# Attention outputs kept chunk by chunk, and their tail columns stored from a small copied tile

## The chip, the core and the metric

The kernel runs on one core of a Trainium2 chip. The core has TensorE (PE: matmuls; PEld: the loads of the stationary operand), VectorE (DVE), ScalarE (ACT), GpSimd (POOL) and SyncE (SP), each with its own queue of instructions, and 16 DMA engines that serve the transfers which SP, ACT and POOL issue. The metric is the device time of the whole program in microseconds. Three runs of the kernel before gave 4875.46, 4877.3 and 4885.39 us; the median is 4877.3 us.

## The reference

Four layers act on x of 2048 rows by 640 columns: A, B, A, B, each added to x after a layer norm. Layer A is the one that the change touches. It cuts the rows into 64 segments of 32, puts 8 memory rows in front of each, and runs attention with 32 heads of 192 columns over the 40 rows; the outputs of the memory rows are the memory of the next segment, so that the segments follow one another:

```python
for s in range(n_seg):
    h = jnp.concatenate([mem, xs], axis=1)          # 8 + 32 rows
    q, k, v = (einsum('btd,dhe->bhte', h, W) for W in (Wq, Wk, Wv))
    p = softmax(where(mask, q @ k.T * scale, -1e9))
    o = einsum('bhte,hed->btd', p @ v, Wo)          # 40 rows of 640
    mem = o[:, :M, :]
    outs.append(o[:, M:, :])
```

Layer B is a linear attention with learned features; it is not changed, apart from the rows of layer A that it finishes at its start.

## The kernel before, in words

**Two parts of a layer A.** A_pre computes queries, keys and values for the last 8 rows of every segment at once and leaves them in DRAM (kqb, vb). A_chain then walks through the 64 segments with the other 32 rows (8 memory rows and 24 rows of x). Each segment has four rounds of 8 heads (NR = 4, L = 3). A round needs Q, K and V of the 32 rows (project, L940: 20 matmuls each, in four column tiles of the array), takes the last 8 rows' columns from DRAM, and computes scores, weights (E), their sums, and attend.

**What a round holds.** The 8 heads are split into two groups, G. A round's attention output is six chunks of 128 partitions, and each chunk has 80 columns: 64 for the 32 rows of the two groups ("main"), 16 for their last 8 rows ("tail"). By the parity of the round the order is main then tail or tail then main, so that a round's new tail columns don't fall where the last round's are still in use.

**OT.** scale_out (L1007) divides attend's result in PSUM by the sums and writes OT, in three VectorE instructions: L1012 for the chunks 0 to 3 (128 x 320 elements) and L1016 twice for the halves of chunks 4 and 5 (64 x 160). OT is `[P, 96, 6]`: slots (columns) outside, the six chunks inside, so that neighbours of one chunk lie six elements apart. Of its 96 slots a round writes 80, from slot 16 or from slot 0 by parity; the main columns are always slots 16 to 79, the tail is 80 to 95 or 0 to 15. There is one OT.

**Who reads OT.** wo_round (L1023) multiplies the main columns by Wo: 12 steps of four matmuls, steps 0 to 7 with the chunks 0 to 3, steps 8 to 11 with the chunks 4 and 5; all four rounds of a segment accumulate in one PSUM tile, W. store_tail (L1018) sends the 16 tail slots to DRAM (otb) in a DMA that GpSimd issues straight from OT. to_raw (L945) also borrows OT's main slots, as a place for the raw K of round 0, before the transposes spread it.

**The tail's V rows.** extra_v (L921) is a DMA, issued by GpSimd, from vb into 16 rows of Vp; attend reads all 96 rows of Vp, so an attend waits until it has landed, and it is issued once the attend before is done.

**The order in a segment** is written out by hand (L1060 to L1160, manual schedule). On TensorE: Q0, K0, Q1, V0, scores 0, K1; then for n = 1, 2: Q(n+1), sums, attend(n-1), scores(n), K(n+1), V(n), and for n = 1 wo_round 0; then V3, sums, attend 2, scores 3, wo_round 1, sums, attend 3, wo_round 2, wo_round 3. scale_out of round n - 1 stands on VectorE between the transposes of Q(n+1) and K(n+1) (for n = 2 behind those of K). On GpSimd, in one queue: extra_v, the four copies and the load of kqb for the next round (L910 to L919), store_tail, and once a segment the store of the rows of the segment before (attn, L906) and the load of the next rows (xr, L890). At a segment's end 25 single-column weight loads (L1035) fill TensorE, VectorE transposes the memory rows of W into hT (L1158, L1159), and the next segment's Q0 begins. The attends of a segment are counted 0 to 3 here.

**The tail's product with Wo** follows in layer B: post_steps fetches otb for 16 segments, spread (L1174) lays each round's tail out as 12 chunks of 128 columns in two copies, one on VectorE and one on ScalarE, and multiply runs the matmuls. The first spreads run while the last segment of the chain is still under way.

Of the kernel before, what the change touches and what calls it, by code (L numbers as in the profile page):

```python
# [8 lines left out]
P = 128  # L9
BF16 = mybir.dt.bfloat16  # L10
F32 = mybir.dt.float32
ACT = mybir.ActivationFunctionType
ALU = mybir.AluOpType
# [102 lines left out]
class Kernel:  # L116
# [746 lines left out]
    def A_chain(self, xn_dram, at_dram, li, load_slot, piece, load_wo, late_wo, wo_mid, wo_end, low):  # L863
        nc, tc, KC, NSEG = self.nc, self.tc, self.KC, self.NSEG
        scale = float(self.Dh) ** -0.5
        NR = 4
        with tc.tile_pool(name=f"A{li}_ch", reuse_waits="tile", bufs=1) as sp, \
# [3 lines left out]
            KT = sp.tile([P, 6, 96], BF16, name="KT")  # L871
            QT = sp.tile([P, 2, 4, 80], BF16, name="QT")
            Vs = sp.tile([P, 896], BF16, name="Vp")
            OT = sp.tile([P, 96, 6], BF16, name="OT")
            for i, t in enumerate((KT, QT, Vs)):
                (nc.vector if i % 2 else nc.gpsimd).memset(t[:], 0.0)
            at_rows = self.attn_rows
# [1 line left out]
            def rounds(s):  # L879
                return range(NR) if s % 2 == 0 else range(NR - 1, -1, -1)  # L880
# [40 lines left out]
            def extra_v(s, n):  # L921
                r = rounds(s)[n]
                t = 64 + 16 * (n % 2)
                nc.gpsimd.dma_start(out=Vs[t:t + 16, :], in_=self.vb_d[s, r].rearrange("g t f -> (g t) f"))  # L924
# [18 lines left out]
                        load_slot(m, order[NR - 1], b)  # L943

            def to_raw(ps, spare):  # L945
                raw = OT[:, 16:80, :].rearrange("p q c -> p (q c)") if spare else sp.tile([P, 384], BF16, name="raw", tag="raw")[:, :]
                nc.scalar.activation(out=raw, in_=ps[:, 0:384], func=ACT.Copy)  # L947
                return raw

# [54 lines left out]
                                         stop=(k == 192), skip_group_check=True)  # L1004
                return O

            def scale_out(O, rc, n):  # L1007
                q0 = 16 - 16 * (n % 2)
                dst = OT[:, q0:q0 + 80, :].rearrange("p q c -> p c q")
                rv = rc[:, :].rearrange("p (x e q) -> p x e q", e=2, q=80)  # L1010
                ov = O[:, 0:480].rearrange("p (c q) -> p c q", q=80)
                nc.vector.tensor_tensor(out=dst[:, 0:4, :], in0=ov[:, 0:4, :],  # L1012
                                        in1=rc[:, :].rearrange("p (c q) -> p c q", q=80), op=ALU.mult)
                for e in range(2):
                    h = slice(64 * e, 64 * e + 64)
                    nc.vector.tensor_tensor(out=dst[h, 4:6, :], in0=ov[h, 4:6, :], in1=rv[h, :, e, :], op=ALU.mult)  # L1016

            def store_tail(n, s, r):  # L1018
                q0 = 80 - 80 * (n % 2)
                nc.gpsimd.dma_start(out=self.otb_d[s, :, 96 * r:96 * r + 96],  # L1020
                                    in_=OT[:, q0:q0 + 16, :].rearrange("p q c -> p (q c)"))

            def wo_round(W, r, first, last):  # L1023
                w = wo_end[:, :] if r in (0, 3) else wo_mid[:, 7680 * (r - 1):7680 * r]
                for i in range(12):
                    G, c = (i // 4, i % 4) if i < 8 else (i % 4 // 2, 4 + i % 2)
                    for g in range(4):
                        nc.tensor.matmul(W[32 * g:32 * g + 32, 0:160], lhsT=OT[:, 16 + 32 * G:48 + 32 * G, c],  # L1028
                                         rhs=w[:, 640 * i + 160 * g:640 * i + 160 * g + 160], start=(first and i == 0),
                                         stop=(last and i == 11), tile_position=(0, 32 * g), skip_group_check=True)  # L1030

# [26 lines left out]
            W = None  # L1058
            for s in range(NSEG):
                order = rounds(s)  # L1060
                L = NR - 1

                def q_or_k(m, n):
                    ps = pqp.tile([P, 512], F32, name="ps_qk", tag="qk")
                    project(hT, ps, m, n, s)
                    return to_raw(ps, m == "K" and n == 0)

                def values(n, pool, tag):
                    pv = pool.tile([P, 512], F32, name="ps_v", tag=tag)
                    project(hT, pv, "V", n, s)  # L1070
                    return pv

                def tails_after(n):
                    if n + 2 < NR:
                        extra_v(s, n + 2)
                    elif s + 1 < NSEG:
                        extra_v(s + 1, n + 2 - NR)

                raw = q_or_k("Q", 0)
                if s > 0:  # L1080
                    io = keep_rows(W)
                to_rows(raw, "Q")
                if s == 0:
                    fill(FILL[li])
                to_rows(q_or_k("K", 0), "K")
                if s == 0:
                    late_wo(2)
                if s > 0:
                    store_rows(s - 1, io)
                W = pop.tile([P, 512], F32, name="ps_w", tag="w")  # L1090
                raw = q_or_k("Q", 1)
                pv = values(0, pop, "v")
                v_rows(pv, 0, "s")
                v_rows(pv, 1, "s")
                S = scores(0)
                to_rows(raw, "Q", 1)
                next_kq(s, 0)
                E = weigh(S)
                to_rows(q_or_k("K", 1), "K")
                if s + 1 < NSEG:  # L1100
                    xr = load_rows(s + 1)
                for n in range(1, L):
                    raw = q_or_k("Q", n + 1)
                    sums(S, E)
                    O = attend(E)
                    tails_after(n - 1)
                    S1 = scores(n)
                    rc = reciprocals(S)
                    E = weigh(S1)
                    S = S1  # L1110
                    to_rows(raw, "Q", n + 1)
                    next_kq(s, n)
                    if n == L - 1:
                        to_rows(q_or_k("K", n + 1), "K")
                        scale_out(O, rc, n - 1)
                    else:
                        rawk = q_or_k("K", n + 1)
                        scale_out(O, rc, n - 1)
                        to_rows(rawk, "K")
                    store_tail(n - 1, s, order[n - 1])  # L1120
                    pv = values(n, pop, "v")
                    v_rows(pv, 0, "s")
                    v_rows(pv, 1, "s")
                    if n < L - 1:
                        wo_round(W, order[n - 1], n == 1, False)
                        if n == 1:
                            load_wo(order[L])
                            if s == NSEG - 1:
                                load_wo(3, low[:, 0:7680])
                pv = values(L, pqp, "qk")  # L1130
                sums(S, E)
                O = attend(E)
                tails_after(L - 1)
                S1 = scores(L)
                next_kq(s, L)
                rc = reciprocals(S)
                E = weigh(S1)
                v_rows(pv, 1, "v")
                v_rows(pv, 0, "s")
                wo_round(W, order[L - 2], False, False)  # L1140
                sums(S1, E)
                O1 = attend(E)
                tails_after(L)
                if s + 1 < NSEG:
                    hT = new_hT()
                    hx_transpose(hT, xr)
                scale_out(O, rc, L - 1)
                store_tail(L - 1, s, order[L - 1])
                wo_round(W, order[L - 1], False, False)
                rc = reciprocals(S1)  # L1150
                scale_out(O1, rc, L)
                wo_round(W, order[L], False, True)
                store_tail(L, s, order[L])
                fill(SEG_FILL)
                if s + 1 < NSEG:
                    wt = sp.tile([P, KC, 32], F32, name="wt", tag="raw")
                    for b0, b1 in ((2, 5), (0, 2)):
                        nc.vector.transpose(out=wt[:, b0:b1, :], in_=W[:, 0:160].rearrange("p (j b) -> p b j", b=KC)[:, b0:b1, :])  # L1158
                        nc.vector.tensor_copy(out=hT[:, b0:b1, 0:8], in_=wt[:, b0:b1, 0:8])  # L1159
            store_rows(NSEG - 1, keep_rows(W))  # L1160

    def post_steps(self, ops):

        nc = self.nc
# [9 lines left out]
        def spread(tb, ot):  # L1174
            o = 7680 + 12288 * (tb % 2)
            ow = low[:, o + 6144:o + 12288].rearrange("p (c q) -> p c q", q=P)
            for k in range(4):
                o5 = ow[:, 12 * k:12 * k + 12, :].rearrange("p (c g) (s t) -> p g c s t", g=2, t=8)
                i5 = ot[:, :, 96 * k:96 * k + 96].rearrange("p s (g t c) -> p g c s t", g=2, c=6)
                for g in range(2):  # L1180
                    self.ev.copy(out=o5[:, g], in_=i5[:, g], eng="vs"[g])
            return ow

        def multiply(tb, ow, p0, p1):
# [49 lines left out]
```

## Time and profile before

| What | Value |
|---|---|
| Median of three runs | 4877.3 us |
| The profiled execution, its own time | 4893.74 us |
| Its span, first to last instruction | 4892.0 us |
| Mean granted TensorE clock | 0.873 |
| Busy: PE, DVE, ACT, POOL | 3831.1, 2763.4, 1971.6, 1719.9 us |
| OT written on VectorE (L1012 and L1016) | 628.8 + 781.7 us |
| One segment of the chain, mean of 126 | 30.60 us |

How to read the lines that follow. In a group of instructions the order is: line of the kernel, engine, operation, output<-inputs with shapes, count | busy us in total, mean ns of one | idle us of the engine just before, and what ended it. In the list of waits it is: engine, tile and line that waited <- what it waited for: us in total, times, longest. In a timeline it is: start us, duration us, engine, line, operation, and in brackets the idle time before and its releaser. In a table of stretches it is: from:to, length, busy us (and instructions) of PE, PEld, DVE, ACT and POOL, granted clock, DMA share, GB/s.

A timeline merges neighbours of one line, so one entry can be two instructions or 48 matmuls, and the durations overlap where an engine starts the next before the last has ended. The granted clock changes between full and half in windows of 3.41 us. The end of a DMA isn't a line of the timeline; it shows as what a later instruction waited for.

### The profile page before, as it was taken

The numbers are of one execution on the slowest core, as the hardware profiler recorded it, in microseconds if no ns is written. First come the engines' busy times: TensorE is split into PE (matmuls) and PEld (weight loads), VectorE is DVE, ScalarE is ACT, GpSimd is POOL, SyncE is SP. The second block draws the span as 40 slices with busy tenths as digits, with TensorE's granted clock in tenths as the row PEclk, the third lists the DMA queues.
The fourth block names the chain that finished last, engine by engine and source line by source line (L and its number), as shares of the span: only waits on it lengthen the run. The fifth ranks groups of instructions, "written<-read, shape, count | busy, mean of one in ns | idle before, by whom it ended". The sixth has DMA issues, their size and how long they took to land.

```text
span 4892.0 us, 167816 instructions
## 1 busy us (share of the span) xinstructions
PE 3831.1 (78%) x69306; PEld 2480.7 (51%) x72670; DVE 2763.4 (56%) x5448; ACT 1971.6 (40%) x4405; POOL 1719.9 (35%) x4359
## 2 busy tenths in 40 slices
PE   9877777777777777788898777777777777777888
PEld 7544444444454444455466544444444544444554
DVE  5455555555555555556633555555555555555555
ACT  2343343433334333345433444434434444433453
POOL 3333333333333333332242333333333333333310
PEclk9988888888888888889999898888888888888899
DMA  9866666666656555570277566666666666666700
GB/s 296 290 199 199 199 199 198 199 199 199 198 196 200 189 190 194 191 254 23 98 226 243 198 214 197 200 201 199 199 197 200 199 199 199 200 199 199 235 8 22
DMA packets 539947, 934.62 MB, mean 191 GB/s; under 512 B 149554, under 2 KB 307978, under 8 KB 539194
## 3 DMA queue, kind: packets, MB, share of 16 engines
q1 hardware_dynamic: 428858, 818.87, 49.8%
q0 software_dynamic: 76672, 91.77, 6.9%
q10 hardware_dynamic: 33664, 13.24, 1.1%
q8 instruction: 558, 9.14, 0.8%
q14 instruction: 195, 1.60, 0.1%
HBM read 853.72 MB, written 73.40 MB: 190 GB/s over the span
## 4 chain that ended last, share of the span: by engine, by line
issue 29%; PE 25%; POOL 15%; DMA 13%; DVE 9%; ACT 5%; PEld 3%; POOLq 0%; DVEq 0%; SPq 0%; ACTq 0%
DMA Vp<-vb 9%; PE ps_qk L940 8%; DVE OT L1016 6%; PE ps_pre L825 3%; POOL kqb L910 3%; POOL otb L1020 2%; PE ps_o L1002 2%; POOL Vp L924 2%; PEld L1035 2%; DMA attn<-orow 2%; PE ps_w L1028 2%; PE ps_pre L849 1%; POOL KT L919 1%; POOL QT L916 1%; PE ps_qk L391 1%
## 5 line engine op out<-in xcount | busy, mean ns | idle before, releaser
L940 PE MATMUL ps_qk<-arena,hT 128*32 128x384 bf16 x20480 | 1184.8, 385 | 80.7 <-PE L1035 75.7
L940 PEld LDWEIGHTS <-hT 128*32 128x32 bf16 x30720 | 862.1, 109 | 631.9 <-issue 262.2
L1028 PE MATMUL ps_w<-arena,OT 128*32 128x160 bf16 x24576 | 729.6, 269 | 355.0 <-DVE OT L1012 244.3
L947 ACT ACTIVATE raw<-ps_qk 128x384 bf16<-128x384 f32 x896 | 439.2, 490 | 1365.5 <-PE ps_qk L940 1153.5
L1028 PEld LDWEIGHTS <-OT 128*32 128x32 bf16 x24576 | 541.4, 131 | 528.6 <-DVE OT L1012 322.5
L956 DVE STREAM_TRANSPOSE QT<-raw 128x256 bf16<-128x256 bf16 x512 | 228.1, 446 | 1015.3 <-PE ps_s L977 749.2
L1016 DVE TENSOR_TENSOR OT<-ps_o,rc 64x160 bf16<-64x160 f32 x1024 | 781.7, 763 | 13.8
L1012 DVE TENSOR_TENSOR OT<-ps_o,rc 128x320 bf16<-128x320 f32 x512 | 628.8, 1228 | 151.7 <-ACT rc L994 75.1
L1002 PE MATMUL ps_o<-E,Vp 96*128 96x80 bf16 x4096 | 248.1, 209 | 519.9 <-DMA Vp<-vb 463.6
L1020 POOL DMA_DIRECT2D otb<-OT x512 | 281.8, 550 | 922.0 <-DVE OT L1016 898.5
L940 PE MATMUL ps_v<-arena,hT 128*32 128x384 bf16 x10240 | 540.6, 354 | 10.6 <-DMA arena<-in_A_Wv_dram 10.6
L1002 PEld LDWEIGHTS <-Vp 96*128 96x128 bf16 x4096 | 201.9, 103 | 595.9 <-ACT rc L994 267.5
L964 ACT ACTIVATE Vp<-ps_v 64x384 bf16<-64x384 f32 x896 | 433.2, 483 | 117.4 <-PE ps_v L940 90.1
L924 POOL DMA_DIRECT2D Vp<-vb x512 | 258.2, 504 | 535.3 <-PE ps_o L1002 520.1
L994 ACT ACTIVATE rc<-ps_s 128x320 f32<-128x320 f32 x512 | 223.9, 437 | 358.2 <-DVE OT L1016 348.7
L910 POOL DMA_DIRECT2D kqb<-kqb x512 | 292.5, 571 | 158.7 <-POOL KT L919 150.2
L983 ACT ACTIVATE E<-ps_s 96x320 bf16<-96x320 f32 x512 | 220.1, 430 | 294.7 <-PE ps_s L977 291.2
L952 DVE STREAM_TRANSPOSE KT<-raw 128x384 bf16<-128x384 bf16 x384 | 222.1, 578 | 185.6 <-ACT raw L947 181.7
L977 PE MATMUL ps_s<-QT,KT 128*96 128x80 bf16 (+1 forms) x3072 | 259.2, 225 | 8.1 <-DVE KT L952 0.9
L993 ACT ACTIVATE ps_s<-ps_s 128x320 f32<-128x320 f32 x512 | 218.7, 427 | 110.8 <-PE ps_s L988 105.6
L977 PEld LDWEIGHTS <-KT 128*96 128x96 bf16 x3072 | 236.5, 131 | 39.2 <-issue 32.2
L906 POOL DMA_DIRECT2D attn<-orow x128 | 93.0, 726 | 406.3 <-ACT orow L902 405.9
(149 smaller groups left out, 4603.0 us busy)
## 6 DMA issues: line engine op xcount, KB each, us to landing
arena<-wo_rows SPq DMA_DIRECT2D x792, 320.0 KB, 5.5
arena<-in_A_Wq_dram SPq DMA_DIRECT2D x427, 384.0 KB, 4.4
arena<-in_A_Wv_dram SPq DMA_DIRECT2D x427, 384.0 KB, 6.2
arena<-in_A_Wk_dram SPq DMA_DIRECT2D x768, 192.0 KB, 5.0
kqb<-kqb POOLq DMA_DIRECT2D x512, 48.0 KB, 4.3
arena<-in_A_Wk_dram SPq DMA_DIRECT2D x43, 384.0 KB, 7.0
vb<-arena POOLq DMA_DIRECT2D x128, 112.0 KB, 6.0
Vp<-vb POOLq DMA_DIRECT2D x512, 28.0 KB, 4.1
```

The costliest lines, as they stand in the source:

```text
L910: nc.gpsimd.dma_start(out=kqb[:], in_=self.kqb_d[s, :, r, :])
L924: nc.gpsimd.dma_start(out=Vs[t:t + 16, :], in_=self.vb_d[s, r].rearrange("g t f -> (g t) f"))
L940: nc.tensor.matmul(ps[32 * g:32 * g + 32, 0:384], lhsT=hT[:, b, :], rhs=rhs, start=(i == 0), stop=(i == KC - 1), tile_position=(0, 32 * g) ...
L947: nc.scalar.activation(out=raw, in_=ps[:, 0:384], func=ACT.Copy)
L956: nc.vector.transpose(out=QT[:, :, 0:4:3, q:q + 64], in_=rv[:, :, 0:3:2, :])
L964: nc.scalar.activation(out=o, in_=i, func=ACT.Copy)
L977: nc.tensor.matmul(S[0:96, c0:c0 + 80 * (q1 - q0)], lhsT=KT[:, 3 * x + i, :], rhs=QT[:, x, q0:q1, :], start=False, stop=(x == 1 and i == 2 ...
L1002: nc.tensor.matmul(O[:, 80 * c:80 * c + 80], lhsT=Vs[0:96, 448 * x + k:448 * x + k + 128], rhs=E[0:96, 160 * x + 80 * e:160 * x + 80 * e + ...
L1012: nc.vector.tensor_tensor(out=dst[:, 0:4, :], in0=ov[:, 0:4, :], in1=rc[:, :].rearrange("p (c q) -> p c q", q=80), op=ALU.mult)
L1016: nc.vector.tensor_tensor(out=dst[h, 4:6, :], in0=ov[h, 4:6, :], in1=rv[h, :, e, :], op=ALU.mult)
L1020: nc.gpsimd.dma_start(out=self.otb_d[s, :, 96 * r:96 * r + 96], in_=OT[:, q0:q0 + 16, :].rearrange("p q c -> p (q c)"))
L1028: nc.tensor.matmul(W[32 * g:32 * g + 32, 0:160], lhsT=OT[:, 16 + 32 * G:48 + 32 * G, c], rhs=w[:, 640 * i + 160 * g:640 * i + 160 * g + 16 ...
```

## The change

OT becomes `[P, 6, 80]`: chunks outside, the round's 80 columns inside, so that each chunk is a run of 80. The three instructions of scale_out write runs. The main columns now begin at column 0 or 16 of a run by parity (m0 in wo_round), and the tail at 64 or 0. A round's tail is now inside the area that the next round writes. The tail is no longer contiguous, so GpSimd copies its 6 x 16 columns to a tile of 96 elements per partition (otb, one buffer), and the DMA goes from there. The raw K of round 0 goes to the buffer of rc, now widened in its type but not in bytes. The tail's order in DRAM becomes chunk, group, row, so that spread needs one copy of 12 chunks per round and not two of 6; the copies take turns on the two engines.

```diff
-            OT = sp.tile([P, 96, 6], BF16, name="OT")
+            OT = sp.tile([P, 6, 80], BF16, name="OT")
...
             def to_raw(ps, spare):
-                raw = OT[:, 16:80, :].rearrange("p q c -> p (q c)") if spare else sp.tile([P, 384], BF16, name="raw", tag="raw")[:, :]
+                w, tag = (640, "rc") if spare else (384, "raw")
+                raw = sp.tile([P, w], BF16, name="raw", tag=tag)[:, 0:384]
...
-            def scale_out(O, rc, n):
-                q0 = 16 - 16 * (n % 2)
-                dst = OT[:, q0:q0 + 80, :].rearrange("p q c -> p c q")
+            def scale_out(O, rc):
...
-                nc.vector.tensor_tensor(out=dst[:, 0:4, :], in0=ov[:, 0:4, :],
+                nc.vector.tensor_tensor(out=OT[:, 0:4, :], in0=ov[:, 0:4, :],
                                         in1=rc[:, :].rearrange("p (c q) -> p c q", q=80), op=ALU.mult)
                 for e in range(2):
                     h = slice(64 * e, 64 * e + 64)
-                    nc.vector.tensor_tensor(out=dst[h, 4:6, :], in0=ov[h, 4:6, :], in1=rv[h, :, e, :], op=ALU.mult)
+                    nc.vector.tensor_tensor(out=OT[h, 4:6, :], in0=ov[h, 4:6, :], in1=rv[h, :, e, :], op=ALU.mult)
 
             def store_tail(n, s, r):
-                q0 = 80 - 80 * (n % 2)
-                nc.gpsimd.dma_start(out=self.otb_d[s, :, 96 * r:96 * r + 96],
-                                    in_=OT[:, q0:q0 + 16, :].rearrange("p q c -> p (q c)"))
+                q0 = 64 - 64 * (n % 2)
+                ob = sp.tile([P, 96], BF16, name="otb", tag="otb")
+                nc.gpsimd.tensor_copy(out=ob[:, :].rearrange("p (c q) -> p c q", q=16), in_=OT[:, :, q0:q0 + 16])
+                nc.gpsimd.dma_start(out=self.otb_d[s, :, 96 * r:96 * r + 96], in_=ob[:, :])
 
-            def wo_round(W, r, first, last):
+            def wo_round(W, n, r, first, last):
+                m0 = 16 * (n % 2)
...
-                        nc.tensor.matmul(W[32 * g:32 * g + 32, 0:160], lhsT=OT[:, 16 + 32 * G:48 + 32 * G, c],
+                        nc.tensor.matmul(W[32 * g:32 * g + 32, 0:160], lhsT=OT[:, c, m0 + 32 * G:m0 + 32 * G + 32],
...
-                o5 = ow[:, 12 * k:12 * k + 12, :].rearrange("p (c g) (s t) -> p g c s t", g=2, t=8)
-                i5 = ot[:, :, 96 * k:96 * k + 96].rearrange("p s (g t c) -> p g c s t", g=2, c=6)
-                for g in range(2):
-                    self.ev.copy(out=o5[:, g], in_=i5[:, g], eng="vs"[g])
+                self.ev.copy(out=ow[:, 12 * k:12 * k + 12, :].rearrange("p c (s t) -> p c s t", t=8),
+                             in_=ot[:, :, 96 * k:96 * k + 96].rearrange("p s (c t) -> p c s t", t=8))
```

The calls of scale_out and wo_round change their arguments and nothing else; their order stays.

More of the change, by code (lines that the diff above doesn't have):

```diff
@@ L1114, in A_chain @@
                         to_rows(q_or_k("K", n + 1), "K")
-                        scale_out(O, rc, n - 1)
+                        scale_out(O, rc)
                     else:
                         rawk = q_or_k("K", n + 1)
-                        scale_out(O, rc, n - 1)
+                        scale_out(O, rc)
                         to_rows(rawk, "K")
@@ L1124, in A_chain @@
                     if n < L - 1:
-                        wo_round(W, order[n - 1], n == 1, False)
+                        wo_round(W, n - 1, order[n - 1], n == 1, False)
                         if n == 1:
@@ L1139, in A_chain @@
                 v_rows(pv, 0, "s")
-                wo_round(W, order[L - 2], False, False)
+                wo_round(W, L - 2, order[L - 2], False, False)
                 sums(S1, E)
@@ L1146, in A_chain @@
                     hx_transpose(hT, xr)
-                scale_out(O, rc, L - 1)
+                scale_out(O, rc)
                 store_tail(L - 1, s, order[L - 1])
-                wo_round(W, order[L - 1], False, False)
+                wo_round(W, L - 1, order[L - 1], False, False)
                 rc = reciprocals(S1)
-                scale_out(O1, rc, L)
-                wo_round(W, order[L], False, True)
+                scale_out(O1, rc)
+                wo_round(W, L, order[L], False, True)
                 store_tail(L, s, order[L])
```

## The prediction

> **What bounds the kernel now.** I read the page first, then the waits, the groups by shape, one end of a segment as a timeline, and a table of clock windows. The page:
>
> ```profile
> span 4892.0 us, 167816 instructions
> PE 3831.1 (78%) x69306; PEld 2480.7 (51%) x72670; DVE 2763.4 (56%) x5448; ACT 1971.6 (40%) x4405; POOL 1719.9 (35%) x4359
> issue 29%; PE 25%; POOL 15%; DMA 13%; DVE 9%; ACT 5%; PEld 3%; POOLq 0%; DVEq 0%; SPq 0%; ACTq 0%
> DMA Vp<-vb 9%; PE ps_qk L940 8%; DVE OT L1016 6%; PE ps_pre L825 3%; POOL kqb L910 3%; POOL otb L1020 2%; PE ps_o L1002 2%; POOL Vp L924 2%; PEld L1035 2%; DMA attn<-orow 2%; PE ps_w L1028 2%; PE ps_pre L849 1%; POOL KT L919 1%; POOL QT L916 1%; PE ps_qk L391 1%
> ```
>
> No engine is full; the chain hops between a small DMA (Vp<-vb), TensorE, VectorE's OT and GpSimd. So a change is worth what it takes from the wait that ends last, and the busy sum of VectorE says little. The waits name two families in front of TensorE:
>
> ```profile
> PE ps_o L1002 <- DMA Vp<-vb: 463.6, 280, 4.1
> ACT rc L994 <- DVE OT L1016: 348.7, 236, 1.9
> PE ps_w L1028 <- DVE OT L1012: 244.3, 265, 1.3
> PE ps_w L1028 <- DVE OT L1016: 102.2, 222, 0.5
> ```
>
> I then averaged the start times in the trace over the 126 segments of the two recurrent chains that follow one another without a break (30.60 us each, 3855 us of the span). In each, attend 1 and attend 2 start 0.14 us after the tail rows of V land (5th to 95th percentile 0.136 to 0.17 us), and attend 3 does in most (0.14 at the median, 0.55 at the 95th). Their mean starts are 15.72, 21.77 and 25.15 us after the segment's start. So two thirds of a segment is paced by a DMA that GpSimd issues after the previous attend, not by VectorE. Only from attend 3 to the end does OT set the pace.
>
> **What the change does to OT's writes.** The groups by shape:
>
> ```profile
> L1016 DVE TENSOR_TENSOR OT<-ps_o,rc 64x160 bf16<-64x160 f32 x1024 | 781.7, 763 | 13.8
> L1012 DVE TENSOR_TENSOR OT<-ps_o,rc 128x320 bf16<-128x320 f32 x512 | 628.8, 1228 | 151.7 <-ACT rc L994 75.1 <-ACT Vp L964 41.7 <-issue 24.6
> L425 DVE TENSOR_TENSOR arena<-ps_v,rk 128x320 bf16<-128x320 f32 x128 | 54.2, 485 | 5.2 <-PE ps_v L421 2.9
> L524 DVE TENSOR_TENSOR arena<-ps_num,arena 120x512 bf16<-120x512 f32 x40 | 26.2, 686 | 11.0 <-ACT arena L523 8.8 <-PE ps_num L518 2.0
> L919 POOL COPY KT<-kqb 128x96 bf16<-128x96 bf16 x512 | 134.6, 263 | 31.6
> ```
>
> L425 has L1012's shape, and L524 its operand kinds (PSUM f32 times SBUF f32 into bf16). Only the output differs: OT is written every sixth element, those two densely. L1012 takes 1228 ns where L425 takes 485. The line through 485 at 320 and 686 at 512 elements gives 318 ns at 160, where L1016 takes 763. VectorE overlaps neighbours (L425 starts 0.40 us apart), so one scale_out (L1012 and two L1016), 2.51 us by the timeline, becomes about 1.0. Bounds: 2.51 if the stride isn't the cause, 0.85 if the overlap is full. I take 1.0.
>
> **Part by part, in one segment.**
>
> *scale_out 0* (round 0). wo_round 0 stalls 0.70 us for L1012 and 0.50 for L1016, both mean values; both go. But attend 1 still waits for its DMA, issued at 9.38 us behind the load of xr on GpSimd, which waits for the DMA of the rows of the segment before. Neither knows OT. The 1.20 us moves into the idle stretch before attend 1 (1.62 becomes 2.82 us). Worth 0. If the DMA were not last there, it would be worth 1.20. The load of wo_end, which SP issues as wo_round 0 frees it, starts 0.7 to 1.2 us sooner; the DMA engines are then full (share 1.01, 360 GB/s), so it waits in its own queue, and I cost it 0.
>
> *scale_out 1 and its tail.* GpSimd's store of tail 1 stands in the queue in front of the V DMA that attend 3 needs. That DMA is issued 0.697 us after attend 2 ends, against 0.29 to 0.30 after attends 1 and 3, so 0.40 is the store's doing. The store ends at 22.48 now. Afterwards scale_out 1 ends near 20.2, the copy takes 0.26 (the L919 row: 96 elements in runs of 16), the hand-over from copy to DMA 0.30 (L910 behind L919), the issue 0.55: done near 21.4, before attend 2 ends at 22.28. Gain 0.33 of the 0.40.
>
> *scale_out 2, copy 2, scale_out 3.* The end of one segment now:
>
> ```profile
> 1288.84 0.74 PE L1002 MATMUL ps_o<-E,Vp 96*128 96x80 bf16 x8
> 1289.52 2.03 PE L1028 MATMUL ps_w<-arena,OT 128*32 128x160 bf16 x48
> 1289.88 0.51 POOL L924 DMA_DIRECT2D Vp<-vb  x1 [1.05 <-PE ps_o L1002]
> 1291.32 1.22 DVE L1012 TENSOR_TENSOR OT<-ps_o,rc 128x320 bf16<-128x320 f32 x1 [0.57 <-ACT rc L994]
> 1292.25 1.56 DVE L1016 TENSOR_TENSOR OT<-ps_o,rc 64x160 bf16<-64x160 f32 x2
> 1292.60 2.02 PE L1028 MATMUL ps_w<-arena,OT 128*32 128x160 bf16 x48 [1.05 <-DVE OT L1012]
> ```
>
> Call the end of attend 3 A. On average scale_out 3 starts at A+1.39, held by the weights that wo_round 2 reads from OT and by rc, which waits for scale_out 2 (the 348.7 us above). The last matmul of wo_round 3 ends at A+4.62. Afterwards rc is early, and a new wait appears: OT no longer alternates its tail, so scale_out 3 waits for copy 2, which stands behind the V DMA (A+0.30 to A+0.81) and ends at A+1.08. What is queued behind the waiting scale_out 3 on VectorE are the transposes of W, which need wo_round 3 anyway. scale_out 3 starts at A+1.15 with the full clock, at A+1.35 with half (when wo_round 2's matmuls hold it). wo_round 3 starts 0.50 later and runs 1.05 unbroken at full clock, 1.81 at half (both lengths stand in the trace for a round that waits for nothing): it ends at A+2.70 or A+3.66. GpSimd has a second new wait: copy 3 needs the one otb buffer, so store 2 must have landed (2.1 us). Behind it stand store 3 and the next segment's row store, wanted 3.0 us into that segment: hidden. If that cover went, xr and then the V DMA would be late.
>
> *The clock.* The clock rows, one window each:
>
> ```profile
> 1209.81:1213.22 3.41, 2.22 (x76) 1.34 (x68) 2.70 (x4) 1.15 (x3) 2.71 (x8) 1.00 1.01 336
> 1213.22:1216.63 3.41, 1.58 (x32) 1.18 (x32) 0.21 (x1) 1.57 (x4) 0.51 (x2) 0.99 1.00 335
> 1216.63:1220.05 3.42, 3.42 (x52) 1.71 (x48) 2.50 (x6) 1.31 (x4) 1.41 (x5) 0.51 0.74 269
> 1230.29:1233.70 3.41, 2.80 (x60) 2.13 (x89) 1.90 (x6) 0.00 (x0) 0.54 (x1) 0.50 0.03 7
> 1233.70:1237.11 3.41, 3.41 (x48) 1.70 (x44) 1.24 (x4) 1.18 (x3) 0.72 (x1) 0.51 0.86 250
> ```
>
> The second column is PE busy, the third from the right the granted clock. A window with TensorE busy 1.58 of 3.41 us is followed by half clock; one with 2.22 isn't; in half clock 2.80 isn't enough to return. Over the chains: under 0.45 busy always drops the clock, over 0.60 never; from half clock, under 0.80 never returns, over 0.90 nearly always. Here the Trainium skill speaks otherwise ("TensorE: Matmul & The Clock Gate", "What's actually happening" and "Why this matters for your kernels"): the clock falls after an idle window of about 3.4 us, so gaps up to about 3 us are harmless. By that rule the 2.82 us before attend 1 is free and nothing but 1.4 to 2 us of gain follows. By the rows it drops the clock for a window in most segments (41% have half clock near 18.5 us now), and where it drops before attend 1, TensorE can reach attend 2 later than its DMA (slack 1.62 us; one half-clock window costs 1.7). I go by the rows: a loss of 0.30. The same rows pay at the end: the tail now has stretches of 1.7 and 0.5 us without matmuls and is at half clock in 70% of segments, and 89% start that way. Segments that start at full clock are 0.9 us shorter (29.8 against 30.7). Afterwards the gaps in the tail are 0.65 and about 0.95 us, 53% busy in the worst window, so I take half clock in 35% of tails and 40% of starts: tail end A+3.04, a gain of 1.58, and 0.49 times 0.9 = 0.45 at the start.
>
> *The rest.* raw for K of round 0 moves from OT to rc's buffer, free since scale_out 3: 0. wo_round's weight loads lose their stride; a round of 48 is paced by its matmuls: 0, at most 0.1. spread does 8 copies of 1536 elements on each of two engines per layer in place of 16 of 768 (692 and about 1240 ns each), under the last segment and under the earlier multiply: 0, within 5 us.
>
> **Sum.** 0.33 + 1.58 + 0.45 - 0.30 = 2.06 us a segment, 127 times (126 unbroken segments, and half for each chain's first and last): 262 us. The profiled execution is 4893.74 us, its span 4892.0; it would be 4632. It lies 16.4 us above the median of the runs, 4877.3, so the prediction is **4615 us**.
>
> **Rivals.**
> 1. *The clock takes it back.* The longer gap before attend 1 always drops it, and the tail stays at half: 0.30 + 0.96 - 0.36 = 0.90 us, 115 us, 4762. For it: no return below 0.80 busy; against: a tail at half clock becomes nearly unbroken work, which returns it.
> 2. *The clock stays full* through tail and start: 0.35 + 1.92 + 0.80 = 3.07 us, 390 us, 4487. Against: 53% busy is at the edge.
> 3. *The layout isn't why OT is slow.* Then the triple stays at 2.51, the copy puts 0.56 us between scale_out 1 and the V DMA, worth 0.35 where it now costs 0.40: 44 us slower, 4921. It decides once the triple stays above 2.3 us, where the tail's gain equals that. Against: L425 and L524.
> 4. *Copy 2 takes the stall's place.* It stands between attend 3 and scale_out 3, its price c after A+0.81. Each microsecond over 0.3 delays the segment's end by one; slower than before from c = 2.3 us. At 2.8 us it would be 0.5 a segment, 4940. Against: 263 ns for KT.
>
> **How the numbers follow.** My case 0.62 (own range 4545 to 4700), rival 1 0.16, rival 2 0.14, rival 3 0.03, rival 4 0.05 (0.03 of it slower). From 4510 to 4750 leaves out rivals 3 and 4, a third of rival 1 and half of rival 2: about 0.2. A measurement of this kernel tells about 0.2% from no change. Faster 0.92, same 0.02, slower 0.06.
>
> **What would show it.** L1012 near 485 ns and L1016 near 318; no wait of ps_w on OT at round 0, and a longer one of ps_o on Vp; the V DMA after attend 2 issued 0.3 us behind it; copy 2 straight behind the V DMA, near 0.26 us; segments near 28.5 us; more full clock at segment starts, less near 18 us. Wrong if attend 1 or 2 starts later than its landing in many segments, if the copies take far over 0.3 us, or if V's DMA lands later.

## The result, and the profile after

The changed kernel takes 4485.62 us (median of four runs, 4471.29 to 4504.94) against 4876.38 us (median of four, 4870.7 to 4885.39) for the kernel before. The ratio is 0.92, with a 95% interval from 0.9153 to 0.9246: 391 us faster, where 262 were forecast, and below the range's end of 4510. The direction was right and the size was wrong by a half: the median lies on the rival "the clock stays full" (4487 us).

The page of the profiled execution (4504.94 us, the slowest of the four; the one profiled before took 4893.74, longer than any of its four) in the lines that answer to those of before:

```profile
span 4503.2 us, 167897 instructions
PE 3573.0 (79%) x69290; PEld 2370.5 (53%) x72670; DVE 2024.2 (45%) x5432; ACT 1960.0 (44%) x4389; POOL 1862.2 (41%) x4871
PE 14%; DMA 11%; POOL 8%; issue 8%; DVE 4%; ACT 2%; PEld 2%; POOLq 0%; SPq 0%; ACTq 0%; DVEq 0%
```

VectorE has 739 us less to do, and GpSimd 142 more. TensorE's busy time fell by 258 us although it does the same matmuls, while the mean granted clock rose from 0.873 to 0.908. Not all of them got shorter: one matmul of Q or K took 353 ns in the mean after 385, and one of V 373 after 354.

The groups by shape, of the changed kernel (the selected lines). L1011 and L1015 are the former L1012 and L1016, L1020 is the new copy and L1021 the store's DMA:

```profile
L1015 DVE TENSOR_TENSOR OT<-ps_o,rc 64x160 bf16<-64x160 f32 x1024 | 324.6, 317 | 13.8
L1011 DVE TENSOR_TENSOR OT<-ps_o,rc 128x320 bf16<-128x320 f32 x512 | 251.8, 492 | 266.3 <-POOL otb L1020 208.0 <-PE ps_w L1029 24.4 <-POOL QT L917 18.9
L1020 POOL COPY otb<-OT 128x96 bf16<-128x96 bf16 x512 | 137.9, 269 | 463.3 <-DVE OT L1015 254.0 <-DVE hT L1160 97.6 <-DMA otb<-otb 66.4
L1021 POOL DMA_DIRECT2D otb<-otb x512 | 283.0, 553 | 173.5 <-POOL otb L1020 147.6 <-issue 25.9
```

The reader is to see three durations and two new waits: 492 ns (forecast 485), 317 (318) and 269 (263), scale_out waiting for the copy of the tail before it (208.0 us in total), and the copy waiting in part for the store before it to land (66.4 us).

The waits of TensorE and of GpSimd, same kernel:

```profile
PE ps_o L1003 <- DMA Vp<-vb: 630.7, 295, 7.8
POOL Vp L924 <- PE ps_o L1003: 621.9, 332, 9.1
DVE OT L1011 <- POOL otb L1020: 208.0, 123, 3.8
```

The wait for the V rows in front of attend grew from 463.6 to 630.7 us, which is the net of two changes. In front of attend 1 it grew from 184.8 to 464.9 us; the stall of wo_round 0, 152 us before, went there as forecast. In front of attend 2 it fell from 169.9 to 65.2 us. Of the 346.5 us in which wo_round waited for OT before, 88.3 are left, nearly all at wo_round 3:

```profile
L1029 PE MATMUL ps_w<-arena,OT 128*32 128x160 bf16 x24576 | 550.8, 241 | 96.5 <-DVE OT L1011 88.3 <-DMA arena<-wo_rows 8.1
```

Here is the end of one segment of the changed kernel as a timeline (lines that don't bear on it are left out):

```profile
1281.77 0.67 DVE L1015 TENSOR_TENSOR OT<-ps_o,rc 64x160 bf16<-64x160 f32 x2
1282.40 0.45 PE L1003 MATMUL ps_o<-E,Vp 96*128 96x80 bf16 x8 [0.68 <-DMA Vp<-vb]
1282.53 0.44 ACT L995 ACTIVATE rc<-ps_s 128x320 f32<-128x320 f32 x1 [0.34 <-DVE OT L1015]
1282.78 0.81 PEld L1029 LDWEIGHTS <-OT 128*32 128x32 bf16 x48
1282.78 1.01 PE L1029 MATMUL ps_w<-arena,OT 128*32 128x160 bf16 x48
1283.15 0.51 POOL L924 DMA_DIRECT2D Vp<-vb  x1 [0.42 <-PE ps_o L1003]
1283.65 0.28 POOL L1020 COPY otb<-OT 128x96 bf16<-128x96 bf16 x1
1283.96 0.49 DVE L1011 TENSOR_TENSOR OT<-ps_o,rc 128x320 bf16<-128x320 f32 x1 [1.53 <-POOL otb L1020]
1284.22 0.57 POOL L1021 DMA_DIRECT2D otb<-otb  x1 [0.29 <-POOL otb L1020]
1284.37 0.66 DVE L1015 TENSOR_TENSOR OT<-ps_o,rc 64x160 bf16<-64x160 f32 x2
1284.51 1.04 PE L1029 MATMUL ps_w<-arena,OT 128*32 128x160 bf16 x48 [0.71 <-DVE OT L1011]
```

Attend 3 ends at 1282.85 (A). The copy stands straight behind the V DMA, and scale_out 3 starts 0.03 us after the copy, at A+1.11. wo_round 3 then runs unbroken in 1.04 us, at full clock, and ends at A+2.70.

### The profile page after: what moved, and what is told of

It reads as the page before. It is cut to its first block, busy times and chain, and to the rows that moved or that the text cites. A ratio compares the mean times of both kernels' runs of the same rounds, so it can differ in the third digit from the quotient of the medians.

```text
span 4503.2 us, 167897 instructions
## 1 busy us (share of the span) xinstructions
PE 3573.0 (79%) x69290; PEld 2370.5 (53%) x72670; DVE 2024.2 (45%) x5432; ACT 1960.0 (44%) x4389; POOL 1862.2 (41%) x4871
## 5 line engine op out<-in xcount | busy, mean ns | idle before, releaser
L940 PE MATMUL ps_qk<-arena,hT 128*32 128x384 bf16 x20480 | 1056.9, 353 | 78.8 <-PE L1036 75.7
L948 ACT ACTIVATE raw<-ps_qk 128x384 bf16<-128x384 f32 x1024 | 503.0, 491 | 1074.9 <-PE ps_qk L940 912.9
L1003 PE MATMUL ps_o<-E,Vp 96*128 96x80 bf16 x4096 | 252.3, 211 | 646.0 <-DMA Vp<-vb 630.7
L1029 PE MATMUL ps_w<-arena,OT 128*32 128x160 bf16 x24576 | 550.8, 241 | 96.5 <-DVE OT L1011 88.3
L940 PE MATMUL ps_v<-arena,hT 128*32 128x384 bf16 x10240 | 580.6, 373 | 9.1 <-DMA arena<-in_A_Wv_dram 9.1
L1029 PEld LDWEIGHTS <-OT 128*32 128x32 bf16 x24576 | 434.6, 99 | 193.3 <-DVE OT L1011 157.9
L953 DVE STREAM_TRANSPOSE KT<-raw 128x384 bf16<-128x384 bf16 x512 | 296.2, 578 | 237.6 <-ACT raw L948 229.9
L1011 DVE TENSOR_TENSOR OT<-ps_o,rc 128x320 bf16<-128x320 f32 x512 | 251.8, 492 | 266.3 <-POOL otb L1020 208.0
L1021 POOL DMA_DIRECT2D otb<-otb x512 | 283.0, 553 | 173.5 <-POOL otb L1020 147.6
L1015 DVE TENSOR_TENSOR OT<-ps_o,rc 64x160 bf16<-64x160 f32 x1024 | 324.6, 317 | 13.8
L1020 POOL COPY otb<-OT 128x96 bf16<-128x96 bf16 x512 | 137.9, 269 | 463.3 <-DVE OT L1015 254.0
```

Source lines behind the costliest of these rows:

```text
L940: nc.tensor.matmul(ps[32 * g:32 * g + 32, 0:384], lhsT=hT[:, b, :], rhs=rhs, start=(i == 0), stop=(i == KC - 1), tile_position=(0, 32 * g) ...
L953: nc.vector.transpose(out=KT[:, :, 0:64], in_=raw.rearrange("p (c j) -> p c j", j=64))
L1003: nc.tensor.matmul(O[:, 80 * c:80 * c + 80], lhsT=Vs[0:96, 448 * x + k:448 * x + k + 128], rhs=E[0:96, 160 * x + 80 * e:160 * x + 80 * e + ...
L1011: nc.vector.tensor_tensor(out=OT[:, 0:4, :], in0=ov[:, 0:4, :], in1=rc[:, :].rearrange("p (c q) -> p c q", q=80), op=ALU.mult)
L1015: nc.vector.tensor_tensor(out=OT[h, 4:6, :], in0=ov[h, 4:6, :], in1=rv[h, :, e, :], op=ALU.mult)
L1029: nc.tensor.matmul(W[32 * g:32 * g + 32, 0:160], lhsT=OT[:, c, m0 + 32 * G:m0 + 32 * G + 32], rhs=w[:, 640 * i + 160 * g:640 * i + 160 * g ...
```

## Where the time went, segment by segment

Outside the two recurrent chains nothing changed. 128 segments of 30.71 us and 961 us around them make the span before; 128 of 27.66 us and 963 us make the span after. (These means take all 128 segments, with the first one of each chain, 41.8 and 39.0 us long before, that the 126 of the prediction left out; the mean of the 126 was 30.60.) The chain's 3.05 us a segment times 128 are 390 us, the whole gain. The spread, forecast at 0 within 5 us, lies in those 961 and 963.

The means over these 128 segments, worked out from the start times, the landings and the clock windows in the two traces, in us:

| Stretch of a segment | before | after | difference | forecast |
|---|---|---|---|---|
| start to attend 1 | 15.75 | 14.94 | -0.81 | -0.45 |
| attend 1 to attend 2 | 6.13 | 6.09 | -0.04 | +0.30 |
| attend 2 to attend 3 | 3.40 | 3.04 | -0.36 | -0.33 |
| attend 3 to the end | 5.43 | 3.59 | -1.84 | -1.58 |
| segments at half clock 1.5 us after the start | 0.88 | 0.08 | | 0.40 |
| segments at half clock 1.5 us ahead of the end | 0.72 | 0.16 | | 0.35 |
| segments at half clock 17.5 us after the start | 0.35 | 0.76 | | "most" |

The four forecasts add up to 2.06, the four measured differences to 3.05. Every one of them came out on the gain's side of its forecast, by 0.36, 0.34, 0.03 and 0.26 us.

## The experiments

No kernel was run besides the one before and the changed one. The two traces show durations, waits, landings and clock windows side by side; which of them caused what is argued from that and not shown by an experiment. These questions are left, each with the edit that would tell its answers apart. None of them was tried.

1. *Is it the length of scale_out 3, or of all four?* Repeat the writes of scale_out 3 until it alone lasts 2.5 us again. If the gaps in the tail set the clock, the tail gets longer and the starts go back to half clock; if only VectorE's time counts, the starts stay at full clock. The same for the rounds 0 to 2 alone.
2. *Is the clock worth what the shares make of it?* Leave OT as before and fill the tail's gaps with idle matmuls into a spare bank.
3. *Is the half clock behind attend 1 a loss?* Put idle matmuls into the gap in front of attend 1 of the changed kernel.
4. *Does the copy pay?* Let the DMA take the six runs straight from OT. scale_out 3 would then wait until that store has landed.
5. *Is copy 2 in the way?* Put it ahead of the V DMA in GpSimd's queue (a sketch: copy_tail and store_copied_tail are the two halves of store_tail):

```diff
-                tails_after(L)
...
                 scale_out(O, rc)
-                store_tail(L - 1, s, order[L - 1])
+                copy_tail(L - 1)
+                tails_after(L)
+                store_copied_tail(L - 1, s, order[L - 1])
```

In the timeline above scale_out 2 has ended at 1282.44, and the copy could have started 1.2 us before it did. By the trace the copy is what ends scale_out 3's wait in 123 cases. But scale_out 3 must also wait until wo_round 2 has loaded the last of its weights from OT, at 1283.59 here. Over the 126 segments that load ends at A+0.77 in the mean and scale_out 3 starts at A+1.12. So, as an estimate from these two figures, the edit gains at most 0.35 us a segment, some 44 us in all. The V DMA that it would delay has room: its rows land 6.4 us ahead of the next segment's attend 0 in the mean.

## Why the prediction was right and wrong, by its own steps

**The durations held.** Writing runs took L1011 to 492 ns and L1015 to 317. The dense rows that served as prices (L425 and L524) were 1.5% off at most. That the stride of OT was what made these instructions slow was inferred before; now the same instruction, with the same operands and another layout of its output, has the dense duration. The rival "the layout isn't why OT is slow" is out.

**scale_out 0: the stall moved, as forecast.** In front of attend 1 the wait for V grew by 280 us. The gap before attend 1 was forecast to grow from 1.62 to 2.82 us; it grew to 3.69, since TensorE came to that point earlier from the segment's start as well. "Worth 0" may have been too low all the same: see the mid stretch below.

**scale_out 1 and its store: right in direction, two thirds in size.** The V DMA behind attend 2 was forecast to lose its wait for the store, a gain of 0.33. It is issued 0.45 us after attend 2 in the mean and no longer 0.69, a gain of 0.24: the store still stands in front of it in 25 of 124 segments, after 51. The stretch to attend 3 is 0.36 us shorter all the same. The rest are small terms that the forecast did not have: attend 2 itself takes 0.05 us less, attend 3 follows the landing 0.07 us sooner, and the DMA takes 0.03 us less.

**scale_out 3 and copy 2: right.** The start at A+1.15 was forecast for full clock, the mean is A+1.12; the end of wo_round 3 at A+2.70 for full clock, and the timeline has A+2.70. The mean end is A+2.82, where the sum with its shares of half clock had A+3.04. "Copy 2 takes the stall's place" was right as a mechanism and too dear as a rival: the copy costs 269 ns, far from the 2.3 us at which it would have decided.

**The step that failed is the clock's shares, and with it the mid stretch.** The prediction had the rule from the clock rows and applied it with shares that were mis-sized: half clock in 35% of the tails and 40% of the starts. Measured: 16% and 8%. It argued that the worst window in the tail, 53% busy, sits at the edge. The windows of the changed kernel, around the segment of the timeline (columns as before: PE busy second, granted clock third from the right):

```profile
1268.18:1271.59 3.41, 2.27 (x77) 1.35 (x69) 1.27 (x4) 2.43 (x6) 2.31 (x8) 1.00 0.97 342
1271.59:1275.00 3.41, 0.98 (x19) 0.90 (x23) 0.00 (x0) 0.04 (x1) 0.24 (x1) 1.00 1.04 359
1275.00:1278.42 3.42, 3.42 (x48) 1.88 (x44) 2.20 (x6) 1.11 (x3) 1.70 (x6) 0.50 0.84 308
1278.42:1281.83 3.41, 3.07 (x85) 2.00 (x74) 1.75 (x6) 2.49 (x7) 2.14 (x7) 1.00 0.09 24
1281.83:1285.24 3.41, 2.13 (x98) 1.85 (x101) 1.61 (x6) 0.79 (x2) 1.95 (x5) 1.00 0.13 28
1285.24:1288.65 3.41, 2.81 (x81) 2.17 (x101) 1.73 (x7) 1.18 (x3) 1.29 (x3) 1.00 0.35 92
```

The gap before attend 1 (0.98 us busy of 3.41) costs one window of half clock. That window is full of work, so the clock returns at 1278.42, in time for the end. The tail's window is busy 2.13 of 3.41 us, 62%. In the chains of both traces a full-clock window under 0.45 busy was always followed by half clock, and one over 0.60 hardly ever, as the prediction had read. Few windows fall between. Slide a window of 3.41 us over the tail of each of 124 segments, from attend 2 to 1.5 us into the next segment: the worst position is 42% busy before and 58% after (medians), not 53%, and 54% of the positions before but 8% after have a window under 53%. So the threshold held. The error is that the worst window was taken to be emptier than it is, and its odds for those of many segments.

The size of it: at the start the share that changed is 0.80 in place of 0.49. With the 0.9 us that the prediction read for a start at full clock that makes 0.72, against the 0.81 measured and the 0.45 forecast. In the tail 16% in place of 35% at half clock, at 0.96 us each, are 0.18 of the 0.26 us by which it came out better. Together the shares make 0.45 of the 0.99 us by which the segment beat its sum. The mid stretch makes 0.34, by a term that the sum did not have. The other 0.20 us lie in small parts in the start, the tail and the stretch to attend 3.

**The mid stretch: the loss was there, and something paid it back.** Half clock near 17.5 us rose from 35% to 76%, as forecast. Attend 2 starts 0.51 us after its V rows have landed, not 0.24: a loss of 0.27, where 0.30 was forecast. The start behind the landing that the prediction named as a sign of being wrong is there in 50 of 128 segments, after 7. In addition attend 1 itself takes 0.13 us longer. But the V DMA behind attend 1 lands 4.70 us after its issue and not 5.14, 0.44 sooner, which pays for both. The prediction put the earlier load of wo_end at 0 and left this landing where it was. In the trace this load's first packets come about 0.9 us sooner after the segment's start (12.1 us, not 12.9), and 99% of them have begun by 19.2 us, not 20.3: the weights' stream drains 1.1 us sooner. The V DMA is issued only 0.67 us sooner, so that it meets some 0.4 us less of the stream, about what its flight lost. That is a match of means. Over single segments, the two long first ones left out, the end of the stream and the landing hardly go together (correlation 0.2 before, 0.0 after). Whether the earlier weights let V land sooner stays open.

**What the starts are worth differs along the segment.** At attend 0 it is plain: before, segments that started at full clock reached it 1.77 us sooner than the others. With 0.80 more of the segments starting so, that makes 1.42, and attend 0 does come 1.41 us sooner in the mean. The V DMA behind it comes only 0.99 us sooner, and its rows take 0.20 longer to land, which leaves 0.81 at attend 1. GpSimd stands in front of it: the load of xr waits for the store of the segment before, as the prediction said (132.6 us in all, after 88.9). Further on it isn't settled. In the kernel before, with those two long segments left out, the 14 segments that started at full clock reached attend 2 at 20.84 us, the other 112 at 21.88. In the changed kernel 116 at full clock reach attend 1 at 14.86 and attend 2 at 20.93; 10 at half clock come to attend 1 later (15.51) but to attend 2 at 21.01, and their segments are no longer than the others. So a start at full clock seems to be worth 0.65 us or more by attend 1, part of which the half clock behind it takes back by attend 2. Ten segments are too few to say more.

**The skill's rule and the rows.** The Trainium skill ("TensorE: Matmul & The Clock Gate", "What's actually happening") ties the drop to an idle window of about 3.4 us. In the kernel before a window that was 46% busy dropped the clock too (1.58 of 3.41 us, its longest gap 1.83 us), and 182 of the chains' 196 drops came without a gap of 3 us or more at the window. There the measurement decides. The half clock behind attend 1 in the changed kernel tells the two rules apart less well. By the page's rule and the forecast gap, the loss of 0.30 us would have been put at nothing. But the gap was forecast at 2.82 us and grew to 3.69, more than the 3 us that the prediction took from the page; in the rows above it is 3.57 us. Of the 104 segments with a gap of 3 us or more 90 had half clock behind it, of the other 22 five.

## What to carry to other kernels

Price an instruction by a row of the same shape and operands that differs in one thing, here the stride of the output: 1228 ns for every sixth element, 492 for runs. Then look for the stretch where this engine ends last: at scale_out 0 another wait took over what was saved, scale_out 1 gave about 0.3 us a segment, and scale_out 2 and 3, at the segment's end, gave most of the gain. Where the clock falls with TensorE's busy share per window, count how many windows fall under the threshold over all phases, not what the worst one does. Closing gaps in the tail came with a gain in two places, in the tail itself and in the start behind it.

## What was unexpected

The V rows' DMA of 28 KB took 4.7 to 6.4 us in the mean from issue to landing while weights streamed at 340 to 370 GB/s, and 2.0 us once they had drained; attends 1 and 2 of a segment wait behind the stream, attend 3 after it. The half clock behind attend 1 went with a loss of 0.27 and 0.13 us, and yet attend 1 to attend 2 took 6.09 us with half clock in 76% of the segments, and 6.13 with 35%: a loss that was forecast and came true stays invisible in the total when another wait shrinks by as much.

The total of rival 2, "the clock stays full", was met partly by luck. Its 0.80 at the start and 1.92 in the tail are near the 0.81 and 1.84 measured. But it counted no loss behind attend 1, and that loss was there, paid by the V rows' landing, which no case of the prediction had.
